# Batch 0's mixer rows in a fused attention and mixer kernel: add, transpose and copy per chunk in place of a folded product, and the first blocks in token halves

## The chip, the cores and the metric

The kernel runs on one core of one Trainium2 chip. The metric is device microseconds (us) of one execution; the kernel before takes 274.43 us (median of three runs, 273.88 to 274.5). The profiled span is about 1.8 us shorter than the time of the same execution, so spans are compared with spans and times with times.

Names in the profile: PE is TensorE's matmuls, PEld its weight loads, DVE is VectorE, ACT is ScalarE, POOL is GpSimd, DMA is a transfer.

## The reference, cut to what matters

```python
# attention with k and v averaged over groups of 8 rows: 8 batches, 8 heads, 576 rows, head width 64
k_p, v_p = k.reshape(B,H,72,8,D).mean(3), v.reshape(B,H,72,8,D).mean(3)
attn = softmax(q @ k_p.T / sqrt(D));  x = (attn @ v_p) put as (B, 576, 512)
# mixer: over tokens, then over channels
AT = relu(x.T @ w_tok1)          # 256 hidden per channel
u  = x + (AT @ w_tok2).T
out = u + relu(u @ w_ch1) @ w_ch2   # 1536 hidden: 12 blocks of 128
```

A batch has 576 tokens: four chunks of 128 and a rest of 64. The rests of all batches are handled together at the end. The product with w_ch1 needs u with its channels on the partitions, that is u transposed, `uT`.

## The kernel before

The kernel is a list of steps per batch, put by hand into an order. The head runs batch 0's attention and token product. Then come nine units: unit n does the two channel products of batch n, the steady work of TensorE, and between its matmuls a table slips in steps of later batches. A table's key is the position in the unit. A bare step belongs to batch n+1, `>` to batch n+2, `<` to batch n itself.

```python
def uT_x(kk, c0, c1):                       # steps X0..X3: x half of the folded product
    ...
    nc.tensor.matmul(out=st["uT_ps", kk][:, c * P:(c + 1) * P],
                     lhsT=parts(st["x"][:, c, :])[:, kk], rhs=ident, start=(c == 0), stop=False)
def uT_a(m):                                # steps A0, A1: AT half, 2 x 4 matmuls of 512 columns
    for kk in range(4):
        ps = st["uT_ps", kk]
        nc.tensor.matmul(out=ps, lhsT=parts(st["AT"][:, m, :])[:, kk], rhs=w_tok2[:, m, 0:512],
                         start=False, stop=(m == 1))
        if m == 1:
            (nc.scalar.copy if kk % 2 else nc.vector.tensor_copy)(out=late("uT")[:, kk, :], in_=ps)
def u(c):                                   # two matmuls of 512 columns, then u = product + x
    ...
    nc.vector.tensor_tensor(out=dst, in0=ps, in1=x, op=ALU.add)
def uT(c):                                  # step t<c>: four transposes of u, one copy
    ...
    for kk in range(4):
        nc.tensor.transpose(out=ps[:, kk, :], in_=parts(src)[:, kk], identity=ident)
    nc.vector.tensor_copy(out=dst[:, :, o:o + P], in_=ps)

def unit_steps(n, st):                      # first channel product
    for m in range(NM):                     # 12 blocks
        ps = ps_one.tile([P, 512], FP32, name="p1")
        for kk in range(4):
            nc.tensor.matmul(out=ps, lhsT=w_ch1[:, kk, m * P:(m + 1) * P], rhs=uT[:, kk, :], ...)
            ...
        nc.scalar.activation(out=GT[:, m, :], in_=ps, func=AF.Relu)
        yield
    ...                                     # second product, GT with w_ch2

HEAD = """c0 c1 d8 q0 d1 q1 d5 kp0 kp1 kt0 kp2 e0 o0 kt1 kp3 kt2 o1 q3 q2 ... g01 X1 h4 X2 Xa X3 Xb A0 A1"""
FIRST = {0: "<u1 <u3", 1: "<u2 <u0 k0 lv2", ...}
THIRD = {0: "av1 >V0", 1: ">K1", 3: ">K0", ..., 10: ">Q0 >V1 at0", ..., 26: ">Q3 >kpT", ...}
```

So before, the transposed u of batch 0 is made directly, by linearity: x transposed (16 narrow matmuls against the identity) plus AT with w_tok2 (8 wide ones), summed in the accumulator. u in its other layout, which the final sum needs, is made later.

More letters. `kp0..kp3` pool batch 0's k on TensorE and copy the result out; `kt0..kt2` transpose those copies; `o` and `e` are scores and exponentials. `K0 K1 V0 V1` are the poolings of a later batch's k and v (four heads each) on GpSimd, `k0` and `v0 v1` the same on VectorE, `kpool` on TensorE. `kpT` transposes both pooled halves of k on TensorE, so it needs K0 and K1, not V0 or V1. `av` is the attention product.

The softmax here doesn't subtract the row's maximum and nothing guards it: scores larger than these inputs give would overflow.

## Time and profile before

| | before |
|---|---|
| time, median of 3 | 274.43 us |
| span of the profiled run | 272.2 us |
| TensorE busy | 264.5 us, 97% |
| first pooling of batch 0's k | 7.63 us |
| pooling of batch 0's v | 12.51 us |
| Relu of AT starts | 20.48 us |
| first w_ch1 block of unit 0 starts | 23.19 us |
| TensorE pooling of batch 1's k | 30.07 us |

The profile lists, per instruction group, start, duration, engine, source line, operation, output from input, shapes and count; what stands in square brackets is the idle time of that engine just before, and what ended it (its releaser). The prediction below shows the main lines. Two more matter later, the start of the head's stages, from the timeline of the kernel before:

```profile
7.63 1.08 PE L202 MATMUL p<-kr,ident 72*72 72x128 bf16 x16 [0.97 <-DMA kr<-in_k_dram]
12.51 1.03 PE L224 MATMUL p<-vr,ident 72*72 72x256 bf16 x8 [0.40 <-DMA vr<-in_v_dram]
```

TensorE pools k as soon as it lands, two steps (16 matmuls) in a row, and 4.88 us later it pools v, for which it even waits 0.40 us.

### The profile page before, as it was taken

Reading aid. Unit: us, or ns where it says so; the run is one execution under the profiler, and the core shown is the slowest. Engines: PE = TensorE matmul, PEld = TensorE weight load, DVE = VectorE, ACT = ScalarE, POOL = GpSimd, SP = SyncE. Lnnn points to the kernel's source line nnn. Section 1 sums busy time; section 2 is a strip of 40 time slices with the busy share of each in tenths; the row PEclk is TensorE's granted clock in tenths of the full one; section 3 lists DMA queues with packets and bytes.
Section 4 is the critical chain, followed back from the end, with each engine's and each line's share of the span. In section 5 each row is a group of like instructions: output and inputs, shape, how many; then the busy total and the mean of one; then the engine's idle time right before and its main releaser. Section 6 shows DMA issues by size and latency. Waiting matters only on the chain.

```text
span 272.2 us, 4534 instructions
## 1 busy us (share of the span) xinstructions
PE 264.5 (97%) x1812; PEld 129.6 (48%) x1812; DVE 141.9 (52%) x279; ACT 110.9 (41%) x192; POOL 130.4 (48%) x119
## 2 busy tenths in 40 slices
PE   8899999999999999999999999999999999999994
PEld 3774545444454544544445444544454444444443
DVE  4487777862674754776266537733674161022022
ACT  2443790058306435325632483058304603603700
POOL 8685221999996994899099999300000000000000
PEclk9999999999999999999999999999999999999999
DMA  7999999995648957994499372224133544024024
GB/s 140 200 203 206 205 206 202 224 197 95 101 67 154 209 114 154 146 224 126 79 159 219 97 136 55 69 72 118 39 81 87 121 71 109 0 60 95 2 52 102
DMA packets 40149, 33.99 MB, mean 125 GB/s; under 512 B 16960, under 2 KB 33600, under 8 KB 40128
## 3 DMA queue, kind: packets, MB, share of 16 engines
q0 software_dynamic: 18672, 17.64, 40.9%
q1 hardware_dynamic: 21296, 15.93, 23.7%
q8 instruction: 14, 0.23, 0.3%
q10 hardware_dynamic: 160, 0.13, 0.2%
q14 instruction: 7, 0.06, 0.1%
HBM read 38.86 MB, written 12.45 MB: 189 GB/s over the span
## 4 chain that ended last, share of the span: by engine, by line
PE 89%; ACT 3%; DMA 3%; DVE 2%; POOL 1%; issue 1%; POOLq 0%
PE p L553 33%; PE p L575 32%; PE p L429 6%; PE p L440 5%; PE p L378 3%; DMA vr<-in_v_dram 3%; PE p L276 2%; ACT ex L263 1%; ACT GT L557 1%; PE p L224 1%; PE p L587 1%; PE pt L276 1%; PE p L446 1%; PE pt L458 1%; ACT ex L297 1%
## 5 line engine op out<-in xcount | busy, mean ns | idle before, releaser
L557 ACT ACTIVATE GT<-p 128x512 bf16<-128x512 f32 x108 | 63.9, 598 | 90.5 <-PE p L553 90.2
L575 PE MATMUL p<-w_ch,GT 128*128 128x512 bf16 x420 | 100.1, 379 | 0.0
L553 PE MATMUL p<-uT,w_ch 128*128 128x512 bf16 x384 | 91.8, 379 | 0.1
L553 PEld LDWEIGHTS <-w_ch 128*128 128x128 bf16 x432 | 40.4, 98 | 48.3 <-issue 3.1
L575 PEld LDWEIGHTS <-GT 128*128 128x128 bf16 x420 | 38.4, 98 | 40.4
L561 DVE TENSOR_TENSOR o<-p,u 128x512 f32<-128x512 f32 x32 | 21.9, 685 | 51.9 <-PE p L575 51.9
L449 DVE TENSOR_TENSOR u<-p,x 128x512 bf16<-128x512 f32 x32 | 21.5, 689 | 18.8 <-PE p L440 18.4
L145 POOL TENSOR_TENSOR t<-t 72x512 f32<-72x512 f32 x24 | 30.3, 1263 | 1.9
L144 POOL TENSOR_TENSOR t<-kr 72x1024 f32<-72x1024 bf16 x12 | 25.4, 2119 | 7.6 <-DMA kr<-in_k_dram 6.8
L144 POOL TENSOR_TENSOR t<-vr 72x1024 f32<-72x1024 bf16 x12 | 25.5, 2124 | 0.7
L297 ACT ACTIVATE ex<-p 72x1024 bf16<-72x1024 f32 x20 | 19.3, 1015 | 8.9 <-PE p L276 8.9
L246 DVE STREAM_TRANSPOSE qD<-qb 128x576 bf16<-128x576 bf16 x28 | 20.6, 792 | 0.0
L396 DVE TENSOR_TENSOR x<-p,den 128x512 bf16<-128x512 f32 x28 | 19.4, 692 | 1.0
L440 PE MATMUL p<-AT,w_tok 128*128 128x512 bf16 x64 | 18.2, 379 | 0.2 <-ACT GT L557 0.2
L378 PEld LDWEIGHTS <-ex 72*128 72x128 bf16 x280 | 13.1, 98 | 8.0 <-DVE x L396 0.6
L480 DVE STREAM_TRANSPOSE uT<-v 128x512 bf16<-128x512 bf16 x20 | 12.9, 686 | 6.1 <-DMA v<-mem 6.1
L429 PE MATMUL p<-x,w_tok 128*128 128x512 bf16 x56 | 14.5, 379 | 0.0
L378 PE MATMUL p<-vp,ex 72*128 72x65 bf16 x280 | 14.3, 194 | 0.2 <-ACT ex L263 0.2
L104 POOL DMA_DIRECT2D qb<-in_q_dram x7 | 5.2, 738 | 17.4 <-DVE qD L246 12.9
L390 DVE RECIPROCAL den<-p 128x8 f32<-128x8 f32 (+1 forms) x35 | 7.0, 200 | 12.0 <-PE p L378 11.7
L429 PEld LDWEIGHTS <-w_tok 128*128 128x128 bf16 x70 | 6.8, 98 | 8.4 <-issue 0.3
L86 POOL DMA_DIRECT2D vr<-in_v_dram x10 | 7.7, 773 | 6.3 <-PE p L553 3.3
(109 smaller groups left out, 218.8 us busy)
## 6 DMA issues: line engine op xcount, KB each, us to landing
out_dram<-o SPq DMA_DIRECT2D x70, 128.0 KB, 2.4
kr<-in_k_dram POOLq DMA_DIRECT2D x7, 576.0 KB, 13.3
qb<-in_q_dram POOLq DMA_DIRECT2D x7, 576.0 KB, 6.2
vr<-in_v_dram POOLq DMA_DIRECT2D x7, 576.0 KB, 14.8
w_ch<-in_moe_w_ch_dram POOLq DMA_DIRECT2D x6, 512.0 KB, 13.9
mem<-u SPq DMA_DIRECT2D x10, 256.0 KB, 2.1
v<-mem SPq DMA_DIRECT2D x12, 160.0 KB, 3.6
v<-mem SPq DMA_DIRECT2D x8, 128.0 KB, 3.2
```

The costliest lines, as they stand in the source:

```text
L144: eng.tensor_tensor(out=t4[:, 0:n], in0=t[:, hs, 0:4], in1=t[:, hs, 4:8], op=ALU.add)
L145: eng.tensor_tensor(out=t4[:, 0:n, 0:2], in0=t4[:, 0:n, 0:2], in1=t4[:, 0:n, 2:4], op=ALU.add)
L246: nc.vector.transpose(out=late("qD")[:, g, db].rearrange("m (r j u) -> m u r j", u=2, r=BR), in_=st["qraw"][:, g].rearrange("m (u r d) -> ...
L297: nc.scalar.activation(out=exv[:, a, :, 0:8 * BP], in_=main[a][0:SP], func=AF.Exp, scale=scale)
L378: nc.tensor.matmul(out=halves[h // 4][:, (h % 4) * (D + 1):(h % 4 + 1) * (D + 1)], lhsT=st["ex"][:, h * S + n0:h * S + n0 + P], rhs=st["vp ...
L429: nc.tensor.matmul(out=ps, lhsT=w_tok1[:, c if c < 4 else 4 + par, m * P:(m + 1) * P], rhs=st["x"][:, c, :] if c < 4 else st["xt"], start= ...
L440: nc.tensor.matmul(out=ps, lhsT=w_tok2[:, m, c * P:(c + 1) * P], rhs=st["AT"][:, m, :], start=(m == 0), stop=(m == 1))
L449: nc.vector.tensor_tensor(out=dst, in0=ps, in1=x, op=ALU.add)
L553: nc.tensor.matmul(out=ps, lhsT=w_ch1[:, kk, m * P:(m + 1) * P], rhs=uT[:, kk, :], start=(kk == 0), stop=(kk == 3))
L557: nc.scalar.activation(out=GT[:, m, :], in_=ps, func=AF.Relu)
L561: nc.vector.tensor_tensor(out=o_sb, in0=ps, in1=(u_tails if n == B else st["u"])[:, c, :], op=ALU.add)
L575: nc.tensor.matmul(out=pss[c], lhsT=GT[:, m, c * P:(c + 1) * P], rhs=w_ch2[:, m, :], start=(m == 0), stop=(m == NM - 1))
```

## The change

The intent: drop the eight wide matmuls of the AT half (their work is done again by the u matmuls), and make uT from u, chunk by chunk. So that TensorE can start on the channel product when only two chunks of uT are there, the first four blocks are done in token halves of 256. The steps of the head and of all tables were put in a new order with it.

```diff
 def uT(c):
-    ps = ps_tr.tile([P, 4, P], BF16, name="pt")
+    odd = first and c % 2
+    ps = (ps_one if odd else ps_tr).tile([P, 4, P], BF16, name="p1" if odd else "pt")
     ...
-    nc.vector.tensor_copy(out=dst[:, :, o:o + P], in_=ps)
+    (nc.scalar.copy if first else nc.vector.tensor_copy)(out=dst[:, :, o:o + P], in_=ps)
-def uT_x(kk, c0, c1): ...
-def uT_a(m): ...
 # unit_steps
-for m in range(NM):
+def hidden(m, n0, n):
+    ...                        # the same block on tokens n0 .. n0+n
+early = 4 if n == 0 else 0
+for half in range(2):
+    for m in range(early):
+        yield from hidden(m, half * 256, 256)
+for m in range(early, NM):
+    yield from hidden(m, 0, 512)
-HEAD = """... d5 kp0 kp1 kt0 kp2 e0 o0 kt1 kp3 kt2 o1 ... w21Dp ... g01 X1 h4 X2 Xa X3 Xb A0 A1"""
+HEAD = """... d5 kp0 kt0 kp1 kp2 o0 kp3 e0 kt1 kt2 o1 ... w21A ... h4 g01 u0 u1 u2 t0 u3 t1"""
-FIRST = {0: "<u1 <u3", 1: "<u2 <u0 k0 lv2", ...}
+FIRST = {0: "k0 <t2", 1: "<t3", ...}
-THIRD = {0: "av1 >V0", 1: ">K1", 3: ">K0", ... 10: ">Q0 >V1 at0", ...}
+THIRD = {0: ">V0 >K1", 1: ">V1 av1", 3: ">K0", ... 10: ">Q0 at0", ...}
 ...                            # SECOND, FOURTH, LATER: slots moved, no step added or removed
```

Three other things moved: the order of the head's first steps, one of the attention scalings from VectorE to ScalarE (`w21Dp` to `w21A`, with some of the head's other steps in another order around it), and the slots of the later tables.

## The prediction

> **What bounds the kernel now.** I read the page first (engine shares, the slices, the chain), then the tensor engine's waits, then the timeline from 14 to 41 us, where the change lies. Busy shares and slices:
>
> ```profile
> span 272.2 us, 4534 instructions
> PE 264.5 (97%) x1812; PEld 129.6 (48%) x1812; DVE 141.9 (52%) x279; ACT 110.9 (41%) x192; POOL 130.4 (48%) x119
> PE   8899999999999999999999999999999999999994
> PE 89%; ACT 3%; DMA 3%; DVE 2%; POOL 1%; issue 1%; POOLq 0%
> ```
>
> The tensor engine is busy for 97% of the span and is 89% of the chain that ended last; only the first two of forty slices are under 90%. Busy matmul time is no proof of a full engine, so I look at cadence too. The steady stretch is this one:
>
> ```profile
> 26.19 4.05 PE L553 MATMUL p<-uT,w_ch 128*128 128x512 bf16 x18
> ```
>
> 18 matmuls in 4.05 us, of which about 0.16 us is the drain of the last (a single one shows 379 ns against a spacing near 216 ns): (4.05 - 0.16) / 18 = 0.216 us each, no gap. So, after the head, a microsecond of tensor work removed, or of tensor waiting removed, is a microsecond of time. All its waits over the span add up to little:
>
> ```profile
> PE p L202 <- DMA kr<-in_k_dram: 1.0, 1, 1.0
> PE p L224 <- DMA vr<-in_v_dram: 0.4, 1, 0.4
> PE p L440 <- ACT GT L557: 0.2, 1, 0.2
> PE p L378 <- ACT ex L263: 0.2, 1, 0.2
> ```
>
> Now the stage that is changed, end of the head and start of unit 0:
>
> ```profile
> 20.39 0.83 PE L491 MATMUL p<-ident,x 128*128 128x128 bf16 x12
> 20.48 0.60 ACT L420 ACTIVATE AT<-pt 128x512 bf16<-128x512 f32 x1 [3.58 <-PE pt L410]
> 20.60 0.69 DVE L422 TENSOR_SCALAR AT<-p 128x512 bf16<-128x512 f32 x1 [0.49 <-PE p L410]
> 21.14 1.92 PE L499 MATMUL p<-w_tok,AT 128*128 128x512 bf16 x8
> 22.45 1.29 DVE L502 CAST uT<-p 128x512 bf16<-128x512 f32 x2 [1.16 <-PE p L499]
> 22.66 1.07 ACT L502 CAST uT<-p 128x512 bf16<-128x512 f32 x2 [1.58 <-PE p L499]
> 24.25 2.83 DVE L449 TENSOR_TENSOR u<-p,x 128x512 bf16<-128x512 f32 x4
> ```
>
> The reader sees: the x half of the folded product fills the tensor engine while both halves of AT are made (20.5 to 21.3), the AT half (8 wide matmuls) follows at once, and the eight u matmuls lie later, under the casts. And the stage behind it:
>
> ```profile
> 28.64 1.22 DVE L144 TENSOR_TENSOR t<-kr 72x1024 f32<-72x1024 bf16 x1 [1.55 <-DMA kr<-in_k_dram]
> 34.73 1.22 DVE L144 TENSOR_TENSOR t<-vr 72x1024 f32<-72x1024 bf16 x1 [0.93 <-DMA vr<-in_v_dram]
> 39.14 0.42 DVE L150 TENSOR_TENSOR vp<-t 72x256 bf16<-72x256 f32 x1
> 40.06 0.42 PE L378 MATMUL p<-vp,ex 72*128 72x65 bf16 x8 [0.16 <-ACT ex L263]
> ```
>
> Batch 1's k lands at 28.64 and its v at 34.73, whatever the engines do; from v the VectorE needs until 39.14 + 0.42 = 39.56 to finish the pooled v. Batch 1's first attention product starts at 40.06. So a head that is much earlier runs into a floor near 39.6.
>
> **What the Trainium skill says.** "TensorE: Matmul & The Clock Gate", section "Wait — 56ns, not 53.3ns?", gives warm back-to-back spacings of 55.6 ns at 128 columns and 215.7 ns at 512; this trace agrees (0.216 above; 12 narrow ones in 0.83 us less the drain, 0.056 each). "Perfetto Trace Analysis", section "Per-instruction lifecycle: what the profiler-reported window actually captures", says a slice leaves out semaphore wait and propagation; here a consumer starts about 0.04 us after its producer's end (a VectorE cast of uT that ends near 23.15, the first channel matmul at 23.19). "ScalarE: Activation LUTs", section "What ACT_TABLE_LOAD costs", gives 186 ns + 0.833 ns per element for an ACTIVATE: 613 ns at 512 and 399 at 256; the trace has 598 ns for the 512-wide Relu and 0.38 us for a 256-wide exp. "DMA: Bandwidth & Descriptors", section "Issuing engines are not separate DMA queues", says descriptors of one queue start in order; the queue here is busy without a break up to about 58 us at some 205 GB/s, so I take the two landings as fixed.
>
> **The change part by part.**
>
> *Work taken from the tensor engine.* The x half is 16 narrow matmuls against the identity, the AT half 8 wide ones. In their place come 16 narrow transposes of u (the same 16 x 0.056 = 0.89 us). The eight wide u matmuls exist in both kernels; they only move ahead. So the net is the AT half: 8 x 0.216 = 1.73 us less.
>
> *Token halves of the first four blocks.* 16 matmuls of 512 columns become 32 of 256. The 256-wide matmuls of the head's token product follow each other every 0.11 us, so 32 x 0.11 = 3.5 us against 16 x 0.216 = 3.5 us: nothing. ScalarE pays 8 x 0.38 = 3.0 in place of 4 x 0.60 = 2.4 us.
>
> *Copies.* Two VectorE and two ScalarE casts are replaced by four ScalarE copies, which I put at 0.60 us each (the trace's 128x512 bf16 transpose copies take 0.42 us, but on VectorE; ScalarE's 128x288 copy takes 0.40). VectorE loses 1.3 us, and another 0.42 by one attention scaling that the new head moves to ScalarE.
>
> *The new waits.* Worked out by hand from these durations. VectorE runs its ten scalings without a hole from 14.39 to 20.11 us, the last one gating AT. One fewer: the last ends near 19.68. AT0 then runs 20.06 to 20.66 on ScalarE, AT1 20.28 to 20.97 on VectorE, and the tensor engine, having no x product to fill with, waits about 0.6 us. u0's two matmuls end near 21.39; the adds of u0 to u3 follow on VectorE at 0.69 each and end at 22.12, 22.81, 23.50, 24.20. Transposes of u0 at 22.2, copy 22.6 to 23.2; of u1 at 22.9, copy 23.3 to 23.9. The first half block (tokens of chunks 0 and 1) starts near 23.95, against 23.19 of the first block before. From there ScalarE has a queue of copies and half Relus on three one-bank buffers: GT 24.6, copy of u2 25.0, GT 25.5, copy of u3 25.8 to 26.4, then GT after GT. The second halves can start at 26.44, and four blocks are done near 28.2.
>
> *The balance there.* Before, at 26.19 one block and all u work was done, and three more take 12 x 0.216 = 2.59: four blocks at 28.78. So the changed kernel is ahead by about 28.8 - 28.2 = 0.6 us: of 1.73 saved plus some 0.4 of the VectorE chain, about 1.5 goes into new waits.
>
> *How much survives.* The product of batch 1 would be reached about 0.6 us earlier (tensor engine free at 39.9 before, so 39.3), but the pooled v is there only at 39.6. The start moves from 40.06 to about 39.6: 0.45 us kept. The scores' exponentials, on ScalarE without a gap from 33.6 to 40.3 before, start some 0.25 earlier and have one Relu fewer in front of the last, so they no longer are the later of the two. After that the tensor engine is full to the end and its work is the same, so the 0.45 stays. The tables of units 1 to 7 only move slots; since those units wait well under 1 us in all, I give them 0.1 +- 0.3. Total: 0.55 us, 274.43 - 0.55 = 273.9.
>
> **The rivals.**
>
> *The whole 1.73 us arrives.* It would if copies and adds hid under tensor work. Against it: at 20.1 to 24 us the new order gives the tensor engine only eight u matmuls and eight transposes, 2.2 us of work in 3.9 us. With it the time is about 272.7.
>
> *The new chain eats it all.* The add, transpose, copy, product path has three engine changes per chunk where the fold had one, and ScalarE takes copies and eight half Relus in about 5 us, which is about 5.4 us of work with 1.2 of it AT and the first copy. If each link costs 0.1 more than I took, four blocks are done at 28.8 and the time is unchanged, 274.4; with a late kr or vr landing it is 274.8.
>
> *A transfer decides.* If v's landing binds harder than I think, 274.1 to 274.4; if v comes earlier (the new table issues batch 3's k before batch 2's v, but both lie behind batch 1's v in the queue), up to 0.3 more is kept: 273.5. The second channel weights queue behind v: 0.5 MB at 205 GB/s puts their first third at an estimated 37.3 us, and its first use moves from 38.03 to 37.5, so it should not bind.
>
> **Range and chances.** The three runs before spread over 0.6 us, and the rivals within reach lie at 273.4 to 274.5. Predicted 273.9 us, eight in ten between 273.1 and 274.7. Two per cent is 5.5 us; the whole change touches some 8 us of one stage and the tensor work it could save is 1.73, so within 2% has a chance of 0.98, faster 0.01, slower 0.01.
>
> **What would show it.** In the changed profile: no identity product of x; 16 transposes of u between 22 and 25 us; a tensor wait on AT near 0.5 us at 20.1; first half block at 23.9 +- 0.3; the first full block (the fifth) at 28.2 +- 0.3 instead of 28.8; kr and vr landings unmoved within 0.3; batch 1's first attention product near 39.6 with VectorE's pooled v as its releaser instead of ScalarE's exponentials; tensor busy time lower by 1.5 to 2 us with a span only about 0.5 lower. It is wrong if the fifth block begins before 27.7 or after 28.7, if the v landing moves, or if a later unit shows a new wait above 0.3 us.

## The result, and the profile after

The changed kernel takes 273.69 us (median of 6 runs, 272.99 to 274.56), the kernel before in the same rounds 274.17 (273.62 to 274.5). The ratio is 0.9984, with a 95% interval of 0.9962 to 1.0006. Ratios here are the mean time of one kernel's fast runs over that of the other's of the same rounds, so they are not quite the ratio of the medians quoted. That is 0.4 us less, well within 2%, and the interval does not exclude zero.

The removed lines shift the numbering: the first channel product is L553 before and L529 after, its Relu L557 and L533; the lines up to L455 are the same in both; after, L459 are the transposes of u and L460 their copies. The page of the changed kernel, its span, busy shares and chain:

```profile
span 271.9 us, 4559 instructions
PE 262.6 (97%) x1820; PEld 129.8 (48%) x1820; DVE 140.7 (52%) x276; ACT 113.4 (42%) x202; POOL 130.4 (48%) x119
PE 82%; POOL 7%; DVE 4%; ACT 2%; DMA 2%; issue 2%; POOLq 0%
```

TensorE lost 1.9 us of busy time (264.5 to 262.6), the span only 0.3. So about 1.6 us of the saved work went into waits. A second sign: GpSimd, 1% of the chain before, is now 7% of it. TensorE's waits, from the table of waits (us in total, how often, longest); one of 1.2 us for a constant at the start stands in both kernels and is left out:

```profile
PE p L202 <- DMA kr<-in_k_dram: 1.2, 1, 1.2
PE p L529 <- DVE u L449: 0.7, 1, 0.7
PE p L213 <- DVE kpz L205: 0.5, 1, 0.5
PE p L440 <- ACT AT L420: 0.5, 1, 0.5
PE pt L193 <- POOL kp L148: 0.4, 1, 0.4
PE p L313 <- DVE kT L216: 0.3, 1, 0.3
```

The first is the landing of batch 0's k (1.0 before). Two belong to the new chain (0.5 for AT, 0.7 before the first half block), two to the head's first steps (0.5 for the copied k, 0.3 for its transpose), and one, on GpSimd's pooled k, lies far away. Now the timeline of the changed stage:

```profile
7.91 0.64 PE L202 MATMUL p<-kr,ident 72*72 72x128 bf16 x8 [1.16 <-DMA kr<-in_k_dram]
9.06 0.30 PE L213 MATMUL p<-ident,kpz 72*128 72x72 bf16 x4 [0.52 <-DVE kpz L205]
13.04 1.03 PE L224 MATMUL p<-vr,ident 72*72 72x256 bf16 x8
20.72 0.60 ACT L420 ACTIVATE AT<-pt 128x512 bf16<-128x512 f32 x1 [1.75 <-PE pt L410]
21.37 1.55 PE L440 MATMUL p<-AT,w_tok 128*128 128x512 bf16 x6 [0.47 <-ACT AT L420]
23.95 0.58 ACT L460 COPY uT<-p 128x512 bf16<-128x512 bf16 x1
24.59 0.60 PE L529 MATMUL p<-uT,w_ch 128*128 128x256 bf16 x4 [0.67 <-DVE u L449]
25.91 4.20 PE L529 MATMUL p<-uT,w_ch 128*128 128x256 bf16 x30
28.89 1.22 DVE L144 TENSOR_TENSOR t<-kr 72x1024 f32<-72x1024 bf16 x1 [3.92 <-DMA kr<-in_k_dram]
34.93 1.22 DVE L144 TENSOR_TENSOR t<-vr 72x1024 f32<-72x1024 bf16 x1 [0.88 <-DMA vr<-in_v_dram]
39.95 0.42 PE L378 MATMUL p<-vp,ex 72*128 72x65 bf16 x8 [0.16 <-ACT ex L263]
```

Read it against the lines of before. The v pooling at 13.04 comes 0.53 us later than before (12.51), before anything of the intended change has run. The wait of 0.47 us on AT is the one that the x product used to fill. The wait of 0.67 us before the first half block is put down to VectorE's add, but that had been done for a while: the copy of the second chunk on ScalarE ended at 23.95 + 0.58 = 24.53, 0.06 us before the matmul. From there on TensorE has no gap. Batch 1's first attention product comes at 39.95, only 0.11 us earlier than before.

To find where the span went, I cut both timelines at the same six events and the end, all of them on the path: first pooling of k; pooling of v; start of AT's Relu; TensorE's pooling of batch 1's k; the 25th weight load of unit 0's second product; the first one of unit 3's second product; the end. Length of each stretch in us:

| | to k | k to v | v to AT | AT to batch 1's k | to unit 0's second product | to unit 3's second product | to the end |
|---|---|---|---|---|---|---|---|
| before | 7.63 | 4.88 | 7.97 | 9.59 | 17.35 | 84.43 | 140.34 |
| after | 7.91 | 5.13 | 7.68 | 9.22 | 17.23 | 84.39 | 140.37 |
| after, its run among the experiments | 7.38 | 5.17 | 7.69 | 9.21 | 17.41 | 84.43 | 140.35 |

The intended change is the fourth stretch (-0.37). The third (-0.29) I put down to the moved scaling; no run moves that scaling alone, so this is argued and not shown. The second, where only the order of the head's first steps differs, gave 0.25 back. The first is the landing of k, which differs from run to run. The last three hardly moved, although all tables were rearranged and a new wait of 0.4 us stands in the sixth. (Two of the marks are weight loads because some 30 of TensorE's 1,800 matmul records are missing in the profiles of x0, x1, x2, x9 and x10; the weight loads are all there.) Two questions for the chip: is the front's 0.25 real, and does the sixth stretch hide two effects of opposite sign?

### The profile page after: what moved, and what is told of

Same layout as the page of the kernel before. It is cut to its first block, busy times and chain, and to the rows that moved or that the text cites. A ratio compares the mean times of both kernels' runs of the same rounds, so it can differ in the third digit from the quotient of the medians.

```text
span 271.9 us, 4559 instructions
## 1 busy us (share of the span) xinstructions
PE 262.6 (97%) x1820; PEld 129.8 (48%) x1820; DVE 140.7 (52%) x276; ACT 113.4 (42%) x202; POOL 130.4 (48%) x119
## 4 chain that ended last, share of the span: by engine, by line
PE 82%; POOL 7%; DVE 4%; ACT 2%; DMA 2%; issue 2%; POOLq 0%
PE p L559 32%; PE p L529 29%; PE p L429 5%; PE p L440 4%; POOL t L144 3%; PE p L378 3%; DMA kr<-in_k_dram 2%; POOL t L145 2%; PE p L276 2%; ACT ex L263 1%; PE p L224 1%; PE pt L459 1%; PE p L571 1%; PE pt L276 1%; PE p L202 1%
## 5 line engine op out<-in xcount | busy, mean ns | idle before, releaser
L533 ACT ACTIVATE GT<-p 128x512 bf16<-128x512 f32 (+1 forms) x112 | 64.6, 582 | 87.2 <-PE p L529 86.5
L529 PE MATMUL p<-uT,w_ch 128*128 128x512 bf16 (+1 forms) x400 | 92.3, 371 | 0.7 <-DVE u L449 0.7
L529 PEld LDWEIGHTS <-w_ch 128*128 128x128 bf16 x448 | 41.9, 98 | 47.1 <-issue 3.4
L86 POOL DMA_DIRECT2D kr<-in_k_dram x10 | 7.9, 787 | 6.6 <-DVE kp L148 5.4
```

The costliest lines, as they stand in the source:

```text
L529: nc.tensor.matmul(out=ps[:, 0:n], lhsT=w_ch1[:, kk, m * P:(m + 1) * P], rhs=uT[:, kk, n0:n0 + n], start=(kk == 0), stop=(kk == 3))
L533: nc.scalar.activation(out=GT[:, m, n0:n0 + n], in_=ps[:, 0:n], func=AF.Relu)
```

## The experiments

Theory: the new chain gains about 0.65 us up to batch 1's k, as worked out; the new order of the head's first steps costs a quarter of a microsecond; and GpSimd's new order costs what the rearranged tables gain. Rivals: the gain is lost on batch 1's landings and pooled v (the floor of the prediction); or TensorE is not really full later on, so that nothing of the head arrives at the end.

### The changed kernel again, and the old order of the head's first steps, both ways

x0_after is the changed kernel. x1_old_front is the changed kernel with this edit, x2_before_new_front is the kernel before with the reverse:

```diff
-HEAD = """c0 c1 d8 q0 d1 q1 d5 kp0 kt0 kp1 kp2 o0 kp3 e0 kt1 kt2 o1 ...
+HEAD = """c0 c1 d8 q0 d1 q1 d5 kp0 kp1 kt0 kp2 e0 o0 kt1 kp3 kt2 o1 ...
```

> The changed kernel itself, to narrow its interval and to have it beside the others on one chip. Theory (0.3 to 0.5 us gained, of 1.7 saved): ratio to before 0.9982 to 0.999. Rival (a chance of the draw, no gain): 1.000.

> The changed kernel with the order of the first head steps (pooling of batch 0's k, its transposes and first scores) as before. Theory: in the changed kernel the new order of these steps made the tensor engine wait 0.5 us for the cast of kpz and 0.3 us for kT, and reach the pooling of v at 13.04 instead of 12.51; undone, v pooling is at about 12.5 again, the first half block at 24.0 to 24.1 instead of 24.59, the fifth channel block near 28.1, and the first attention product of batch 1 goes from 39.95 to no earlier than 39.6 (v floor): time 0.2 to 0.5 us below the changed kernel's. Rival: k and v landings moved by chance and the order costs nothing: v pooling stays near 13.0 or moves with the k landing only, time unchanged.

> The kernel before with the new order of the first head steps and nothing else. Theory: v pooling starts 0.3 to 0.6 us later than with the old order for the same k landing, and with the fold behind it nothing takes that back: 0.2 to 0.5 us slower than before, ratio 1.001 to 1.002. Rival (order free): ratio 1.000.

Measured, with the kernel before at 274.08 in the same rounds: x0_after 273.6 (273.34 to 274.21), ratio 0.999 (0.9974 to 1.0006); x1_old_front 273.42 (273.03 to 273.83), ratio 0.9979 (0.9965 to 0.9993); x2_before_new_front 274.41 (273.87 to 275.5), ratio 1.0019 (0.9999 to 1.0038). From the timeline of x1_old_front:

```profile
12.29 1.04 PE L224 MATMUL p<-vr,ident 72*72 72x256 bf16 x8 [0.28 <-DVE qT L239]
39.21 0.42 PE L378 MATMUL p<-vp,ex 72*128 72x65 bf16 x8 [0.16 <-DVE vp L150]
105.03 0.30 PE L193 MATMUL pt<-ident,kp 72*128 72x72 bf16 x4 [0.44 <-POOL kp L148]
```

In this run k was pooled from 7.49, so k to v took 4.80 us against 5.17 in x0_after. One part of the expectation failed: the first attention product was to come no earlier than 39.6, and came at 39.21, with batch 1's v taken up at 34.35 and not at 34.93. Over all kernels the split is clean: the seven profiles with the new order have 5.10 to 5.25 us from k to v (after, x0_after, x2, x3, x4b, x5, x7), five with the old order 4.69 to 4.89 (before, x1, x6, x8, x9). Before is among these five although 0.40 us of its stretch is a wait for v. A sixth, x10, took 6.05, because v landed late and was waited for by 1.0 us. The timed ratios of x1 (against x0_after) and of x2 (against before) move in the direction that this says, by 0.3 and 0.5 us, but the times alone do not show it: the intervals of x1 and x0_after overlap, and that of x2 holds 1. The cause can be read from the lines of the changed kernel above: with `kt0` directly behind `kp0`, TensorE has nothing to do while VectorE copies the pooled k out (0.52 us); in the old order `kp1` lies there.

The third line shows one place where a lead ends: at 105.03 TensorE waits 0.44 us for GpSimd. In the profile of x2 the head's token weights landed late (1.2 us waited), and that run was its slowest; its fourth and later stretches are those of before.

### Full blocks instead of token halves, first attempt

```diff
-early = 4 if n == 0 else 0
+early = 0
```

> The changed kernel with its first four channel blocks 512 tokens wide again. The first block must then wait for all four copies of uT: by the durations of the changed trace it starts near 26.9 (copy of chunk 3 would end about 26.0 to 26.4 without half Relus between) instead of 24.59, while the two half blocks done by 25.85 (0.86 us of work) are lost: theory 0.7 to 1.3 us slower than the changed kernel, so slower than before by 0.4 to 0.9. Rival (the halves cost ScalarE what they give): same as the changed kernel within 0.3 us.

The first full block reads chunks 2 and 3 of uT, which are only transposed by table steps behind it. It was mended as x4b_full_blocks below.

### Is the rest full: eight more matmuls; the old tables; the fold without its AT half

x3_extra8 puts eight 128x512 matmuls on a constant tile into unit 3 of the changed kernel. x5_old_tables is the changed kernel with the SECOND to LATER tables of before. x6_no_at_half is the kernel before without the eight matmuls of the AT half, so uT is x transposed alone; its result is wrong (relative error 0.10).

```diff
+    def extra():                       # x3: step X8 in FOURTH, position 34
+        ps = ps_one.tile([P, 512], FP32, name="p1")
+        for _ in range(8):
+            nc.tensor.matmul(out=ps, lhsT=warm[:, 0:P], rhs=warm, start=True, stop=True)
```
```diff
-    ... rhs=ident, start=(c == 0), stop=False)                    # x6
+    ... rhs=ident, start=(c == 0), stop=(c == 3))
-    nc.tensor.matmul(out=ps, lhsT=parts(st["AT"][:, m, :])[:, kk], rhs=w_tok2[:, m, 0:512],
-                     start=False, stop=(m == 1))
```

> The changed kernel with eight more 128x512 matmuls on a constant, in unit 3, far from any load. Theory (tensor engine full behind the head): + 8 x 0.216 = 1.7 us, ratio to before about 1.0048. Rival (there is slack to hide in): less than 0.8 us.

> The changed kernel with the step tables of units 1 to 8 as before. Theory: these tables give nothing: within 0.3 us of the changed kernel. Rival (the gain is in the tables): back at the time of before or above.

> The kernel before with the AT half of the fold left out (8 wide matmuls less, nothing else moved; the result is wrong on purpose). Theory (landings of batch 1's k and v are a floor close behind): the casts of uT come 1.5 us earlier, but the scores of batch 1 can't start before about 32.4 nor its first attention product before 39.6, so only 0.4 to 0.8 us are gained: ratio 0.997 to 0.9985. Rival (saved tensor work is saved time): 1.7 us, ratio 0.9938.

Measured, the kernel before at 274.01 in these rounds:

x3_extra8: 275.28 (275.11 to 275.75), ratio 1.0054 (1.0041 to 1.0067). Its last stretch is 142.09 us against 140.35, 1.74 more, which is eight times 0.217. Past unit 3 a matmul costs its full 0.22 us, and that stretch is 140.33 to 140.37 in every kernel but this one. So TensorE is full there, whatever arrives at it earlier stays, and the rival of a slack rest falls.

x5_old_tables: 273.21 (272.88 to 273.8), ratio 0.9975 (0.9963 to 0.9987), span 271.4. So the new tables of units 1 to 7 do not help the changed kernel. Set against x0_after's 0.999 they would cost it some 0.4 us, but the two intervals overlap, and the profile does not show that much: its sixth stretch is 84.34 us against 84.43.

x6_no_at_half: 274.25 (273.29 to 275.33), ratio 1.0007 (0.9987 to 1.0027). This missed on both sides: the theory had put down a small gain, the rival nearly the whole 1.73 us, and there is none. The timeline of x6_no_at_half shows what took it in the profiled run:

```profile
22.15 0.59 PE L551 MATMUL p<-uT,w_ch 128*128 128x512 bf16 x2 [0.88 <-ACT uT L500]
29.28 1.06 PE L224 MATMUL p<-kr,ident 72*72 72x256 bf16 x8 [0.26 <-DMA kr<-in_k_dram]
31.71 0.30 PE L193 MATMUL pt<-ident,kp 72*128 72x72 bf16 x4 [0.50 <-DVE kp L148]
```

The first line shows half of it: with the eight matmuls gone, TensorE waits 0.88 us for the casts of uT, which before lay largely beneath them. So AT to batch 1's k took 8.75 us, only 0.84 less than before. That was still a lead. But TensorE now stood at that k before it had landed, and VectorE, whose pooling of k starts with the landing and takes 2.4 us, held the transposes for another half microsecond; at 33.43 came 0.20 us more for VectorE's transposed q. The next stretch is 18.43 us against 17.35, and the lead is gone. In this run k's first consumer started at 29.26, later than the 28.64 of before; across the profiles it starts between 27.98 and 30.34. So a landing is a floor, but at another place in each run. That the casts and the landing took the gain in all six timed runs is argued from one profile, not shown.

### Full blocks, GpSimd's order undone, and the change without its reorderings

x4b_full_blocks has `early = 0`, with `t2 t3` at the end of the head and not in the table. x7_v1_back undoes the order of one pair on GpSimd in the changed kernel:

```diff
-THIRD = {0: ">V0 >K1", 1: ">V1 av1", 3: ">K0", ... 10: ">Q0 at0", ...}
+THIRD = {0: ">V0 >K1", 1: "av1", 3: ">K0", ... 10: ">Q0 >V1 at0", ...}
```

x8_old_front_tables takes both the old head front and the old tables, which leaves of the change the new chain, the token halves and the moved scaling.

> The changed kernel without token halves: first four channel blocks 512 tokens wide, the transposes of u's chunks 2 and 3 ahead of them. Theory: the first block waits for all four copies (about 26.3, the copies being back to back without half Relus), 0.86 us of half-block work no longer fills that wait: 0.5 to 1.1 us slower than the changed kernel, that is at or above the time of before. Rival (the halves cost ScalarE what they give): within 0.3 us of the changed kernel.

> The changed kernel with one step of unit 2's table moved back to where it was: GpSimd's pooling of the second half of batch 4's v goes behind the pooling of its k again. Theory: in the changed kernel the tensor engine waits 0.4 to 0.5 us near 105 us for GpSimd's kp, because that pooling stands ahead of k's on GpSimd; moved back, this wait is gone and the time falls by 0.3 to 0.5 us (ratio to before near 0.9975). Rival (the wait is only shifted, GpSimd's chain being the limit either way): the wait reappears within the same batch and the time stays at the changed kernel's 273.6.

> The changed kernel with both the order of the first head steps and the tables of units 1 to 8 as before: what is left is the change proper (u, add, transposes, token halves, the end of the head and unit 0's table). Theory: the tables are worth 0.3 to 0.4 us, the front order 0.1 to 0.3, both cut by the landings of v and the second channel weights near 39 to 43 us: 0.7 to 1.0 us below before, ratio 0.9965 to 0.9975. Rival (the two overlap: any lead ends at the landings): same as with the old tables alone, 0.9975.

Measured, the kernel before at 274.01: x4b_full_blocks 273.99 (273.52 to 274.57), ratio 1.0001 (0.9988 to 1.0015); x7_v1_back 273.04 (272.58 to 273.34), ratio 0.996 (0.9946 to 0.9974); x8_old_front_tables 273.38 (272.71 to 274.02), ratio 0.997 (0.9955 to 0.9984).

With full blocks the first one must wait for all four copies. From the timeline of x4b_full_blocks:

```profile
25.02 4.91 PE L529 MATMUL p<-uT,w_ch 128*128 128x512 bf16 x22 [0.67 <-ACT uT L460]
```

The fourth copy ends at 24.97, well before the 26.3 that was expected. AT to batch 1's k is 9.75 us instead of 9.22, so the token halves are worth 0.53 us, and without them this stretch would be longer than with the fold (9.59).

For x7 look at GpSimd around 100 us. Before, in the timeline of the kernel before:

```profile
96.07 0.72 POOL L148 TENSOR_TENSOR kp<-t 72x256 bf16<-72x256 f32 x1
100.40 0.72 POOL L148 TENSOR_TENSOR kp<-t 72x256 bf16<-72x256 f32 x1
105.20 0.29 PE L193 MATMUL pt<-ident,kp 72*128 72x72 bf16 x4
```

And after:

```profile
95.67 0.72 POOL L148 TENSOR_TENSOR kp<-t 72x256 bf16<-72x256 f32 x1
104.35 0.72 POOL L148 TENSOR_TENSOR kp<-t 72x256 bf16<-72x256 f32 x1
105.12 0.30 PE L193 MATMUL pt<-ident,kp 72*128 72x72 bf16 x4 [0.40 <-POOL kp L148]
```

Those are the last instructions of K1 and K0 of batch 4. Each pooling occupies GpSimd for about 4.33 us (100.40 - 96.07). Before, K0 follows K1 and TensorE finds both 4 us before it needs them. After, V1 lies between, K0 ends at 105.07, and TensorE waits. With V1 put back, x7's pooled k is ready at 100.97 again, the transposes run at 104.79 without a wait, and the sixth stretch falls from 84.43 to 83.80. That is about 0.2 more than the wait that the profile shows, and the reason lies in how a wait is drawn: the slice of the 512-wide matmul before it lasts 0.379 us, while in a full stream the next one would start after 0.216, so 0.16 us of lost time hides under that slice. The sum fits wherever it can be tried: 0.46 + 0.16 = 0.62 here (0.63 by the stretches); 0.40 + 0.16 = 0.56 for the changed kernel's own profile (84.39 - 83.80 = 0.59); 0.19 + 0.16 = 0.35 for the w_ch2 wait in x1 below (17.57 - 17.23 = 0.34), where narrow matmuls stand before it (eight take 0.42 us in the profile, and in a full stream the next starts after 0.26). Against the 84.43 of the kernel before, 0.63 is what the other moved slots gain when nothing holds them back: the 0.3 us that TensorE waited for an exponential near 109 us before, for one, is gone. So the sixth stretch did hide two effects. In time x7 is 0.8 us below x0_after by the ratios (with intervals that just touch). They were run at other times.

x8 says what the change is worth without these two reorderings (it keeps the moved scaling and unit 0's new table): 0.003 x 274 = 0.8 us, with an interval from 0.4 to 1.2. Its profile was its slowest run, with 1.5 us waited for late token weights; its fourth stretch is 9.22 like that of the changed kernel.

### Both repairs together, and GpSimd's order put into the kernel before

x9_front_and_v1 is the changed kernel with the edits of x1 and x7. x10_before_v1_early is the kernel before with `1: ">K1 >V1"` and `10: ">Q0 at0"` in THIRD.

> The changed kernel with batch 4's v pooling back behind k's (as in the run that gained by it) and the first head steps in the old order as well. Theory: the two are independent, but the front order's gain is cut by the landings near 39 to 43 us, so 0 to 0.3 us below the run with v's pooling back alone: ratio to before 0.995 to 0.996. Rival (the front order is free once the landings bind): 0.996 to 0.997, no better.

> The kernel before with only GpSimd's pooling of the second half of batch 4's v moved ahead of the second pooling of its k, as the changed kernel has it. Theory: k is then ready near 105.4 instead of 101.1, the tensor engine comes for it near 105.0, and waits 0.2 to 0.6 us: 0.2 to 0.6 us slower than before, ratio 1.001 to 1.002. Rival (GpSimd's order does not matter): 1.000 and no such wait.

Measured, the kernel before at 274.24: x9_front_and_v1 272.73 (272.48 to 273.31, six runs), ratio 0.995 (0.9936 to 0.9965); x10_before_v1_early 274.65 (274.24 to 275.0), ratio 1.0019 (1.0005 to 1.0032). The page of x9 and two lines of its timeline:

```profile
span 271.0 us, 4528 instructions
80.01 0.18 PEld L193 LDWEIGHTS <-kp 72*128 72x128 bf16 x4 [0.52 <-POOL kp L148]
104.22 0.30 PE L193 MATMUL pt<-ident,kp 72*128 72x72 bf16 x4
```

And x10's timeline:

```profile
105.44 0.72 POOL L148 TENSOR_TENSOR kp<-t 72x256 bf16<-72x256 f32 x1
106.22 0.30 PE L193 MATMUL pt<-ident,kp 72*128 72x72 bf16 x4 [0.19 <-POOL kp L148]
```

x9 is the best version, 1.4 us below the kernel before (0.005 x 274) and with a correct result. The times are those of two repairs that add up: 0.3 us of the front (x1 against x0) and 0.8 of V1 (x7 against x0) make 1.1, on top of x0's 0.3, though each of these carries some 0.4 us of uncertainty. From the first pooling of k on, the profile of x9 is 0.9 us shorter than that of x0_after and 1.2 shorter than that of before. And the same order of V1, put into the kernel before, makes the same wait there (0.19 us, since that kernel arrives later) and a sixth stretch of 84.79 instead of 84.43, longer by 0.19 + 0.16 as above. The cause is the order on GpSimd, not the new head.

The stretches of the runs, in the same order as above:

| | to k | k to v | v to AT | AT to batch 1's k | to unit 0's second product | to unit 3's second product | to the end |
|---|---|---|---|---|---|---|---|
| x1_old_front | 7.49 | 4.80 | 7.69 | 9.22 | 17.57 | 84.69 | 140.35 |
| x2_before_new_front | 7.98 | 5.10 | 8.94 | 9.59 | 17.34 | 84.43 | 140.34 |
| x3_extra8 | 7.61 | 5.10 | 7.68 | 9.22 | 17.23 | 84.40 | 142.09 |
| x4b_full_blocks | 7.20 | 5.13 | 7.69 | 9.75 | 17.22 | 84.39 | 140.36 |
| x5_old_tables | 7.48 | 5.10 | 7.68 | 9.21 | 17.28 | 84.34 | 140.34 |
| x6_no_at_half | 7.87 | 4.69 | 7.97 | 8.75 | 18.43 | 84.41 | 140.35 |
| x7_v1_back | 7.52 | 5.25 | 7.69 | 9.41 | 17.54 | 83.80 | 140.36 |
| x8_old_front_tables | 7.24 | 4.85 | 9.01 | 9.22 | 17.23 | 84.35 | 140.34 |
| x9_front_and_v1 | 7.61 | 4.89 | 7.69 | 9.22 | 17.22 | 84.01 | 140.34 |
| x10_before_v1_early | 7.14 | 6.05 | 7.97 | 9.59 | 17.34 | 84.79 | 140.34 |

x1's gain at the front is lost in the fifth and sixth stretches. Its lead over the changed kernel's profile is 0.75 us at the end of the head (0.42 of it from an earlier landing of batch 0's k), 0.39 after a wait for w_ch2 at 43.10, 0.14 after the transposes of batch 3's k at 80.22, which start 0.06 us after GpSimd has finished pooling it (80.16), and 0.09 after those of batch 4's at 105.03. So GpSimd sets two floors. x9 is free of the one at 105, but it too meets the one at 80 (79.95, then 80.01, the second line above) and loses 0.2 us there, which is why its sixth stretch is 84.01 and not the 83.80 of x7, which comes later. In x7 batch 1's k landed late (its first consumer starts at 29.85), which is the 0.2 us more in the fourth stretch and the 0.3 in the fifth.

## Why the prediction was right or wrong, point by point

The time, 273.9 us with 273.1 to 274.7, held: 273.69, and 273.6 among the experiments. "Within 2%" was right. But part of that is luck: the forecast gain of 0.55 us is of the size of the noise, and the sum behind it has errors that cancel in part, so its steps deserve a look one by one. Three readings were off without weight: before, VectorE does nine scalings and not ten (the tenth, `w30A`, is ScalarE's), and idles 0.18 us among them; the last of the forty slices is under 90% as well; and by the prediction's own figures ScalarE's four copies, eight half Relus and AT make 6.0 us, not 5.4.

**Work taken from TensorE: right.** Put at 1.73 us less; busy time fell by 1.9.

**Copies and half Relus: right.** ScalarE's copy was put at 0.60 us and took 0.58 to 0.61; the half Relu at 0.38 took 0.38 to 0.40. The wait on AT was put at "about 0.6" in the working and near 0.5 as its sign; it was 0.47.

**The new chain, from AT to the first half block: right, almost to the hundredth.** The prediction ran AT0 from 20.06 and the first half block from 23.95, 3.89 us apart. In the profile they are 20.72 and 24.59, 3.87 apart. The two marks themselves failed (23.9 +- 0.3 was the sign given), because the stage started late.

**The fifth block: its length put too high.** It was to start 4.25 us after the first half block; it starts at 28.65, 4.06 after. ScalarE's queue of copies and half Relus, which the prediction worried about, never held TensorE: after 24.59 there is no gap. In the page's profile 28.65 misses 28.2 +- 0.3; in x9, whose v pooling starts at 12.50 as the prediction assumed, AT0 starts at 20.19, the first half block at 24.06 and the fifth block at 28.11.

**The balance of 0.6 us at batch 1's k: right.** The stretches v to AT and AT to batch 1's k give 0.29 + 0.37 = 0.66. x9, with the old front, shows it directly: it pools batch 1's k at 29.41 against 30.07 before, 0.66 earlier. The prediction had split it otherwise: the VectorE scaling at 0.4 was 0.29, and the rest, 1.73 less "about 1.5", so 0.2, was 0.37.

**How much survives: the mechanism failed.** The prediction let the first attention product be stopped by the pooled v near 39.6, so that 0.15 of 0.6 would be lost. The step that failed is "so they no longer are the later of the two": in the changed kernel ScalarE's exponential ends at 39.90 and VectorE's v at 39.77, and the product starts at 39.95, released by the exponential, which moves with TensorE. The interval from batch 1's k to that product is 10.0 us before, after, in x1 and in x9 (10.2 in x0_after): the lead was carried through unchanged. Only in x1 is v the later (39.18, the exponential 39.16), and there too the idle time before the product is the same 0.16 us. Nor does v stay near 39.6: it is ready between 38.79 and 39.77 in the profiles of the changed kernel and its variants. What there is of a floor is the landing of k, as x6 shows, and further on GpSimd's pooled k; the prediction had taken both landings as fixed. They did stay within 0.3 us in the page's profile (28.89 and 34.93), but k's consumer moves by more than 2 us.

**The head's front: the missing term.** The prediction changed nothing before the scalings, "the last ends near 19.68" starting from the same v. The diff showed `kt0` moved ahead of `kp1`, and I did not cost it. It is worth 0.25 us in the two page profiles, and 5.10 to 5.25 us against 4.69 to 4.89 over twelve profiles.

**The tables: right size, wrong reason.** "The tables of units 1 to 7 only move slots; ... I give them 0.1 +- 0.3." The net in the profiles is 0.04 less (84.43 to 84.39). But it is a gain and a loss of about the same size: with V1 put back the stretch is 83.80 (x7) or 84.01 (x9), so 0.4 to 0.6 us shorter than before, and V1's place costs 0.6 to 0.7 (x0_after against x7, x1 against x9). The prediction's own sign for being wrong, a new later wait above 0.3 us, appeared: 0.4 at 105 us. The lag of GpSimd could have been seen beforehand: one pooling takes 4.33 us and TensorE needed K0 about 4 us after it was ready, so a pooling slipped in ahead of K0 uses up that slack.

**The rivals.** "The whole 1.73 us arrives" was rightly set aside: 0.47 and 0.67 us of new waits stand in its place. "The new chain eats it all" fell as well, though x4b shows how close it was: without the token halves, v to batch 1's k takes 17.44 us (7.69 + 9.75) against 17.56 before, and the time is that of before. "A transfer decides" is true in part of x6's profile and of single runs; nothing shows it for the changed kernel's mean.

What stays open: whether x6's gain is lost in the same way in all runs; whether the 0.29 us of the third stretch are the moved scaling's alone; how much of the tables' gain belongs to which moved slot; and whether x5's time is better than x0's by more than noise.

## What to carry to other kernels

Before costing a change for what it is named after, go through the diff for every step that moved, and cost each move: here two moves outside the intended change cost about 1 us (1.1 by the times, 0.9 by the stretches), and undoing them brought the gain from 0.3 to 1.4 us. On a slow engine with long instructions, list who waits for each of them and by how much: V1 could wait, K0 could not, and one slot decided 0.6 us by the stretches. And read a stretch that did not move as a question: cut both timelines at the same events, and undo parts one at a time, since zero can be a sum of two.

## What the Trainium skill lacked or had wrong

- "TensorE: Matmul & The Clock Gate", section "Back-to-back issue gap", gives about 131 ns per matmul at 512 columns and 81 ns at 128 for a sustained stream of weight load and matmul pairs, and calls the single gap of some 216 and 56 ns isolated. Here the stream has the isolated figures: 18 matmuls of 512 columns, each with its own weight load, follow each other every 0.216 us, the 12 narrow ones every 0.056 us, and eight more wide ones cost 1.74 us of span (0.217 each).
- No page says how far the landing of one and the same queued transfer moves between executions. Here the first consumer of batch 1's k starts between 27.98 and 30.34 us over the profiles, and in two of them TensorE waited 1.2 and 1.5 us for token weights that the others did not wait for.
- No page says that an idle gap in TensorE's row is shorter than the time lost. Here it is short by 0.16 us: a gap of 0.46 us was worth 0.63, one of 0.19 us 0.34 to 0.36.
